# One PSUM evacuation of batch 1's convolution moved from VectorE to ScalarE

## The chip, the cores and the metric

The kernel runs on one core of a Trainium2 chip. The metric is the device time of one execution in microseconds. The engines are named as in the profile: PE is TensorE, the matrix engine (PEld its weight loads), DVE is VectorE, ACT is ScalarE, POOL is GpSimd, and SP is the engine that issues most DMAs.

## The reference

The input x is 8 batches of 4224 rows and 192 columns. First a lightweight causal convolution runs along the rows, with 7 taps and one softmax-normalised filter for each of 8 heads (24 columns each). Then a low-rank mixer works on the result:

```python
# attention part: w is softmax of weight over its 7 taps
out = np.einsum('hk,bskhg->bshg', w, x_unf)
# mixer part
xt = x.transpose(0, 2, 1)
h = xt @ U @ V
u = x + h.transpose(0, 2, 1)
ch = np.maximum(u @ w_ch1, 0.0) @ w_ch2
return (u + ch).astype(np.float32)
```

U is 4224x32, V is 32x4224, w_ch1 is 192x768 and w_ch2 is 768x192.

## The kernel before

The rows are cut into tiles of 128: 33 per batch, 264 in all, and 33 groups of 8 tiles. Work on a group has these steps, each with its line:

- The convolution makes y (tile y_sb). It multiplies banded matrices with pieces of x on TensorE and evacuates the PSUM banks to SBUF as bf16. Batches 0 and 1 use `conv` (matmuls L365); from batch 2 on `conv32` is used (matmuls L335). Both evacuate through the helper `evac`, whose ScalarE branch is L252 (an activation with Copy) and whose VectorE branch is L254 (a tensor copy). A string such as "AD" says which engine takes which half: "A" is ScalarE, "D" is VectorE.
- `tt_mm` (L398) contracts y of a whole batch with U; `tt_split` (L412, L413), `tt_sum` (L424) and `tt_done` (L418) bring the result to SBUF.
- `h_group` and `h_tiles` multiply it with V (L453) and VectorE adds y, which makes u (tile u_sb, L475). `transp` (L494) transposes u with a DMA into uT.
- `w1` multiplies uT with the first weight (L550) and evacuates with a ReLU into rl_sb, on ScalarE (L564) or VectorE (L566).
- `w2` multiplies rl_sb with the second weight (L579); VectorE adds u (L588) and SP writes the result out (L596).

All matmul outputs take one of 8 PSUM banks from a single pool (`bank()`), in turn. A bank is used again 8 allocations later, when its evacuation is over.

The order of the work is written out by hand. The list `SLOTS` (L615) gives, for each slot, groups for `w1`, groups for `w2`, and jobs to be placed between the calls of `w2`. No planner or scheduler moves anything. The third slot is `([2], [1], {0: ["d1", "h1"], 1: ["t1"], ...})`: after `w1` of group 2, and ahead of the first `w2` call of group 1, the job "d1" runs the whole convolution of batch 1, and then "h1" runs `h_group(1)`. After that first `w2` call comes "t1", `tt_mm` of batch 1. "s1" and "h4" follow later in the slot, and `w1` of group 3 opens the next slot.

The job "d1" (L761 to L764) loops over the 8 heads. For each head `conv` takes two banks and makes 8 matmuls; the first bank holds rows of 16 tiles (16 times 24 is 384 columns), the second those of 17 tiles (408 columns). The two banks are then evacuated, the first by ScalarE, the second by VectorE. After the last head the transpose of group 3, `transp(3)`, is issued, held back until the last matmul of the convolution.

Of the kernel before, what the change touches and what calls it, by code (L numbers as in the profile page):

```python
# [14 lines left out]
def kernel(  # L15
# [40 lines left out]
    def bank():  # L56
        return psp.tile([P, 512], F32, name="ps", tag="ps")
# [192 lines left out]
    def evac(eng, out, in_):  # L250
        if eng == "A":
            nc.scalar.activation(out=out, in_=in_, func=ACT.Copy)  # L252
        else:
            nc.vector.tensor_copy(out=out, in_=in_)  # L254
# [27 lines left out]
    def x_shift(b):  # L282


        xbt[b] = xbs.tile([P, NB1, D], BF16, name="xb_sb")

        def same(s0, s1, *rest):
            def step():
                nc.gpsimd.tensor_copy(out=xbt[b][:, s0:s1, :], in_=xt[b][:, s0 + 1 : s1 + 1, :])  # L289
                for t0, t1 in rest:  # L290
                    nc.gpsimd.tensor_copy(
                        out=xbt[b][HB : HB + QB, t0:t1, :],
                        in_=xt[b][HB : HB + QB, t0 + 1 : t1 + 1, :],
                    )

            return step

        def ahead(r, s0, s1):
            def step():
                q = slice(HB * r + QB, HB * r + HB)  # L300
                nc.gpsimd.tensor_copy(out=xbt[b][q, s0:s1, :], in_=xt[b][q, s0:s1, :])  # L301

            return step

        m = NB0 // 2
        return [
            same(0, m),
            same(m, NB0, (NB0, NB1)),
            ahead(0, 0, m),
            ahead(0, m, NB0),  # L310
            ahead(1, 0, m),
            ahead(1, m, NB1),
        ]
# [3 lines left out]
    def conv32(b, h0, nh, engs):  # L317


        if yt[b] is None:  # L320
            yt[b] = ys.tile([P, NT, D], BF16, name="y_sb")
        nk = (NB0 // 2, NB1 // 2)
        for n in range(nh):
            h = h0 + n
            hs = slice(h * GS, h * GS + GS)
            pp = [bank(), bank()]
            for cg in range(4):
                t, w, st = (
                    (xt[b], bands[h // HQ][:, h % HQ, QB : 2 * QB], 1 + cg // 2)
                    if cg % 2  # L330
                    else (xbt[b], band2[:, h, :], cg // 2)
                )
                for r in range(2):
                    hr = slice(HB * r, HB * r + HB)
                    nc.tensor.matmul(  # L335
                        out=pp[r][QB * cg : QB * cg + QB, 0 : nk[r] * GS],
                        lhsT=w[hr],
                        rhs=t[hr, st : st + 2 * nk[r] - 1 : 2, hs],
                        start=True,
                        stop=True,  # L340
                        tile_position=(HB * r, QB * cg),
                    )
            for part in range(2):
                j0 = NB0 // 2 * part
                evac(
                    engs[(2 * n + part) % len(engs)],
                    yt[b][:, j0 : j0 + nk[part], hs],
                    pp[part][:, 0 : nk[part] * GS].rearrange("p (k a) -> p k a", a=GS),
                )

    def conv(b, h0, nh, rs, engs, k0=0, k1=NT, pp=None):

        if yt[b] is None:
            yt[b] = ys.tile([P, NT, D], BF16, name="y_sb")
        nk = {r: min(k1, (NB0, NB1)[r] // 2) - k0 for r in rs}
        if pp is None:
            pp = {r: bank() for r in rs}
        w = nh * GS
        for hh in range(nh):
            h = h0 + hh  # L360
            for halo in range(2):
                for r in rs:
                    for c in range(2):
                        st = 1 - halo + c + 2 * k0
                        last = nc.tensor.matmul(  # L365
                            out=pp[r][HB * c : HB * c + HB, 0 : nk[r] * w].rearrange(
                                "p (k a) -> p k a", a=w
                            )[:, :, hh * GS : hh * GS + GS],
                            lhsT=bands[h // HQ][
                                HB * r : HB * r + HB, h % HQ, HB * halo : HB * halo + HB  # L370
                            ],
                            rhs=xt[b][
                                HB * r : HB * r + HB,
                                st : st + 2 * nk[r] - 1 : 2,
                                h * GS : h * GS + GS,
                            ],
                            start=(halo == 0),
                            stop=(halo == 1),
                            tile_position=(HB * r, HB * c),
                        )  # L380
        for n, r in enumerate(rs):
            j0 = NB0 // 2 * r + k0
            evac(
                engs[n % len(engs)],
                yt[b][:, j0 : j0 + nk[r], h0 * GS : h0 * GS + w],
                pp[r][:, 0 : nk[r] * w].rearrange("p (k a) -> p k a", a=w),
            )
        return last
# [3 lines left out]
    def tt_mm(b, js, p=None):  # L392

        if p is None:
            p = bank()
        for n, j in enumerate(js):
            c = n % 4
            nc.tensor.matmul(  # L398
                out=p[32 * c : 32 * c + 32, 0:D],
                lhsT=U_sb[:, j // 4, j % 4, :],  # L400
                rhs=yt[b][:, j, :],
                start=(n < 4),
                stop=(n + 4 >= len(js)),
                tile_position=(0, 32 * c),
            )
        return p

    def tt_split(b, p):

        hi = sml.tile([P, D], BF16, name="tt_hi")  # L410
        lo = sml.tile([P, D], BF16, name="tt_lo")
        nc.scalar.activation(out=hi[:], in_=p[:, 0:D], func=ACT.Copy)  # L412
        nc.vector.tensor_tensor(out=lo[:], in0=p[:, 0:D], in1=hi[:], op=ALU.subtract)  # L413
        ttb[b] += [hi, lo]
# [6 lines left out]
    def tt_sum(b):  # L421
        p = bank()
        for n, part in enumerate(ttb[b]):
            nc.tensor.matmul(  # L424
                out=p[:, 0:D],
                lhsT=R4[:],
                rhs=part[:],
                start=(n == 0),
                stop=(n + 1 == len(ttb[b])),
            )  # L430
        tt_done(b, p)
# [52 lines left out]
    def h_group(g):  # L484
        t0, t1 = g * GT, g * GT + GT
        while t0 < t1:
            b = t0 // NT
            te = min(t1, (b + 1) * NT)
            h_tiles(b, t0 - b * NT, te - b * NT)
            t0 = te  # L490

    def transp(g):
        uTt[g] = uts.tile([P, 4, 3, P], BF16, name="uT")
        return nc.sync.dma_start_transpose(  # L494
            out=uTt[g][:].rearrange("p i c t -> p (i c) t"),
            in_=ut[g][:].rearrange("p i c f k -> p (i c f k)"),
        )
# [100 lines left out]
    def held(ins, after):  # L598
        tc.add_manual_dep(
            ins.ins,  # L600
            after.ins.name,
            mybir.DependencyInfo(mybir.DependencyClass.Sync, mybir.DependencyReason.DATA),
            reason="transfer held back",
        )

    def x_load(b, q, after):
        if q == 0:
            x_tile(b)
            x_zero(b, nc.gpsimd)
        held(x_part(b, *XP[q]), after)  # L610
# [145 lines left out]
    def do(what):  # L756
        if what[0] == "c":
            b, h0, n, engs = what[1:].split(":")
            conv32(int(b), int(h0), int(n), engs)
            return  # L760
        if what[0] == "d":  # L761
            for h in range(H):
                last = conv(int(what[1:]), h, 1, [0, 1], "AD")
            held(transp(3), last)  # L764
            return
        if what[0] == "l":
            b, q = (int(v) for v in what[1:].split(":"))
            x_load(b, q, done_w2[-1])
            return
        if what[0] == "x":  # L770
            b, n = (int(v) for v in what[1:].split(":"))
            steps.extend(x_shift(b))
            for _ in range(n):
                steps.pop(0)()
            return
        n = int(what[1:])
        if what[0] == "h":
            h_group(n)
            if n > 1 and n != 3:
                transp(n)  # L780
        elif what[0] == "t":
            tt_split(n, tt_mm(n, range(NT)))
        else:
            tt_sum(n)
# [55 lines left out]
```

## Time and profile before

| what | value |
|---|---|
| median of 8 runs | 326.55 us (326.29 to 326.89) |
| the profiled execution | 326.5 us |
| its span, first to last instruction | 324.7 us |
| granted TensorE clock, mean | 0.997 |
| instructions | 9590 |
| conv evacuations of batch 1 on ACT (L252, 128x384) | 8, from 38.28 us, 3.19 us together |
| conv evacuations of batch 1 on DVE (L254, 128x408) | 8, from 38.43 us, 4.00 us together |

Times inside the trace count from the first instruction. The profiled execution's own time is 1.8 us longer than its span, for what lies around the span. A line of the timeline has the start in us, the length in us, the engine, the line of the kernel, the operation, what is written and read, the shape and the count; in square brackets stands how long the engine was idle before it and what released it. A line of the groups ends with busy us, mean ns of one, and idle us before them. A line of the waits has who waited for whom, the total in us, how often, and the longest. The chain that ended last is followed back from the last instruction, at each step to what released it.

### The profile page before, as it was taken

The numbers are of one execution on the slowest core, as the hardware profiler recorded it, in microseconds if no ns is written. First come the engines' busy times: TensorE is split into PE (matmuls) and PEld (weight loads), VectorE is DVE, ScalarE is ACT, GpSimd is POOL, SyncE is SP. The second block draws the span as 40 slices with busy tenths as digits, with TensorE's granted clock in tenths as the row PEclk, the third lists the DMA queues.
The fourth block names the chain that finished last, engine by engine and source line by source line (L and its number), as shares of the span: only waits on it lengthen the run. The fifth ranks groups of instructions, "written<-read, shape, count | busy, mean of one in ns | idle before, by whom it ended". The sixth has DMA issues, their size and how long they took to land.

```text
span 324.7 us, 9590 instructions
## 1 busy us (share of the span) xinstructions
PE 318.1 (98%) x3998; PEld 223.9 (69%) x3998; DVE 269.5 (83%) x552; ACT 170.1 (52%) x343; POOL 143.6 (44%) x112
## 2 busy tenths in 40 slices
PE   8999999999999999999999999999999999999994
PEld 3757576478678647866864784597796497497494
DVE  7769999987977986998798699879888888896853
ACT  1766724860874396098249609825804903903900
POOL 8684179729937794685779496000000000000000
PEclk9999999999999999999999999999999999999998
DMA  9999993999996899699889966149077089048044
GB/s 106 192 191 183 210 199 106 197 196 246 219 150 182 222 177 169 165 145 202 189 219 158 216 173 168 51 120 249 26 199 240 3 164 275 2 121 269 2 142 151
DMA packets 122908, 53.52 MB, mean 165 GB/s; under 512 B 87761, under 2 KB 122833, under 8 KB 122865
## 3 DMA queue, kind: packets, MB, share of 16 engines
q1 hardware_dynamic: 84528, 38.08, 47.1%
q0 software_dynamic: 38192, 14.73, 39.8%
q8 instruction: 31, 0.51, 0.7%
q14 instruction: 13, 0.10, 0.1%
q10 hardware_dynamic: 144, 0.10, 0.1%
HBM read 29.49 MB, written 25.95 MB: 171 GB/s over the span
## 4 chain that ended last, share of the span: by engine, by line
PE 94%; DVE 3%; ACT 1%; issue 0%
PE ps L579 42%; PE ps L550 39%; PE ps L335 3%; PE ps L453 3%; PE ps L155 2%; PE ps L398 2%; DVE rl_sb L566 1%; PE ps L365 1%; ACT rl_sb L564 1%; DVE y_sb L254 1%; DVE u_sb L475 1%; PE ps L505 1%; PE ps L520 0%; DVE band L254 0%; PE ps L678 0%; PE ps L424 0%
## 5 line engine op out<-in xcount | busy, mean ns | idle before, releaser
L564 ACT ACTIVATE rl_sb<-ps 128x512 bf16<-128x512 f32 x233 | 124.3, 604 | 108.0 <-PE ps L550 96.0
L579 PE MATMUL ps<-W_sb,rl_sb 128*128 128x192 bf16 x1584 | 141.9, 246 | 0.1
L579 PEld LDWEIGHTS <-rl_sb 128*128 128x128 bf16 x1584 | 128.0, 98 | 13.5 <-issue 13.0
L550 PE MATMUL ps<-uT,W_sb 64*128 64x512 bf16 x1188 | 131.7, 376 | 0.0
L566 DVE TENSOR_SCALAR rl_sb<-ps 128x512 bf16<-128x512 f32 x163 | 105.3, 687 | 15.7 <-PE ps L550 15.4
L550 PEld LDWEIGHTS <-W_sb 64*128 64x128 bf16 x1188 | 66.8, 94 | 60.6 <-issue 4.0
L588 DVE TENSOR_TENSOR out_sb<-ps,u_sb 128x384 f32<-128x384 f32 (+1 forms) x133 | 70.3, 549 | 25.8 <-PE ps L579 25.4
L301 POOL COPY xb_sb<-x_sb 32x3072 bf16<-32x3072 bf16 (+1 forms) x24 | 67.5, 2824 | 0.7
L475 DVE TENSOR_TENSOR u_sb<-y_sb,ps 128x192 bf16<-128x192 bf16 (+1 forms) x168 | 66.2, 460 | 0.0
L289 POOL COPY xb_sb<-x_sb 128x3072 bf16<-128x3072 bf16 x12 | 32.7, 2742 | 36.0 <-PE ps L335 21.5
L252 ACT ACTIVATE y_sb<-ps 128x408 bf16<-128x408 f32 (+4 forms) x89 | 37.8, 513 | 10.4 <-PE ps L335 7.8
L79 POOL DMA_DIRECT2D x_sb<-in_x_dram x32 | 27.0, 847 | 16.2 <-PE ps L550 9.4
L254 DVE CAST y_sb<-ps 128x408 bf16<-128x408 f32 (+4 forms) x37 | 19.7, 577 | 0.8 <-PE ps L365 0.7
L453 PE MATMUL ps<-tt_sb,V_sb 32*128 32x192 bf16 x264 | 12.4, 246 | 0.2 <-DVE y_sb L254 0.2
L335 PE MATMUL ps<-xb_sb,band 64*32 64x384 bf16 x192 | 12.1, 332 | 0.0
L335 PE MATMUL ps<-x_sb,band 64*32 64x384 bf16 x192 | 12.1, 333 | 0.0
L453 PEld LDWEIGHTS <-V_sb 32*128 32x128 bf16 x264 | 4.7, 92 | 7.5 <-issue 7.5
L155 PE MATMUL ps<-zz 128*128 128x512 f32 x12 | 7.5, 778 | 1.5 <-DVE zz L145 1.5
L412 ACT ACTIVATE tt_hi<-ps 128x192 bf16<-128x192 f32 x8 | 2.6, 330 | 11.2 <-PE ps L398 11.1
L365 PE MATMUL ps<-x_sb,band 64*64 64x240 bf16 (+3 forms) x192 | 8.0, 275 | 0.4 <-DVE band L254 0.4
L365 PEld LDWEIGHTS <-band 64*64 64x64 bf16 x192 | 6.0, 106 | 2.2 <-issue 1.2
L335 PEld LDWEIGHTS <-band 64*32 64x32 bf16 x384 | 4.5, 89 | 4.1 <-issue 3.0
(65 smaller groups left out, 72.9 us busy)
## 6 DMA issues: line engine op xcount, KB each, us to landing
out_dram<-out_sb SPq DMA_DIRECT2D x131, 192.0 KB, 3.0
x_sb<-in_x_dram POOLq DMA_DIRECT2D x14, 384.0 KB, 7.6
x_sb<-in_x_dram POOLq DMA_DIRECT2D x7, 432.0 KB, 8.2
x_sb<-in_x_dram POOLq DMA_DIRECT2D x7, 408.0 KB, 8.9
x_sb<-in_x_dram POOLq DMA_DIRECT2D x1, 504.0 KB, 7.5
uT<-u_sb SPq DMA_TRANSPOSE x31, 3.8
x_sb<-in_x_dram POOLq DMA_DIRECT2D x1, 480.0 KB, 5.6
W_sb<-in_moe_w_ch_dram POOLq DMA_DIRECT2D x2, 192.0 KB, 7.6
```

The lines of the kernel that those rows point to most:

```text
L79: return nc.gpsimd.dma_start(out=xt[b][HB * r : HB * r + HB, s0:s1, :], in_=x[b, blk * HB : (blk + s1 - s0) * HB, :].rearrange("(j p) d -> ...
L252: nc.scalar.activation(out=out, in_=in_, func=ACT.Copy)
L289: nc.gpsimd.tensor_copy(out=xbt[b][:, s0:s1, :], in_=xt[b][:, s0 + 1 : s1 + 1, :])
L301: nc.gpsimd.tensor_copy(out=xbt[b][q, s0:s1, :], in_=xt[b][q, s0:s1, :])
L335: nc.tensor.matmul(out=pp[r][QB * cg : QB * cg + QB, 0 : nk[r] * GS], lhsT=w[hr], rhs=t[hr, st : st + 2 * nk[r] - 1 : 2, hs], start=True, ...
L453: nc.tensor.matmul(out=banks[pr][:, a * D : (a + 1) * D], lhsT=V_sb[32 * q : 32 * q + 32, (j // 8) * 2 + j % 2, :], rhs=ttb[b][32 * q : 32 ...
L475: nc.vector.tensor_tensor(out=u_group(g)[:, i : i + n, :, hf, :], in0=yt[b][:, run[0] : run[0] + n, :].rearrange("p n (c k) -> p n c k", c=3),
L550: last = nc.tensor.matmul(out=pps[m][hf][:], lhsT=W1_sb[HB * hf : HB * hf + HB, c, m * P : (m + 1) * P], rhs=uTt[g][HB * hf : HB * hf + HB ...
L564: nc.scalar.activation(out=rl[:, m, hf, :], in_=pp[hf][:], func=ACT.Relu)
L566: nc.vector.tensor_scalar_max(out=rl[:, m, hf, :], in0=pp[hf][:], scalar1=0.0)
L579: last = nc.tensor.matmul(out=cps[:, a * D : (a + 1) * D], lhsT=rlt[g][:, m, hf, (i + a) * P : (i + a + 1) * P], rhs=W2_sb[:, m, :], start ...
L588: nc.vector.tensor_tensor(out=o[:, 0:n, :].rearrange("p n (c k) -> p n c k", c=3), in0=cps[:, 0 : n * D].rearrange("p (n c k) -> p n c k", ...
```

## The change

The call of `conv` inside the job "d1" gets another string for head 2 alone. For that head both halves are evacuated by ScalarE, so that ScalarE takes nine of the sixteen evacuations of batch 1 and VectorE seven.

```diff
         if what[0] == "d":
             for h in range(H):
-                last = conv(int(what[1:]), h, 1, [0, 1], "AD")
+                last = conv(int(what[1:]), h, 1, [0, 1], "AA" if h == 2 else "AD")
             held(transp(3), last)
             return
```

The matmuls, the banks, the order of the heads and the transpose are as they were.

## The prediction

> **What bounds the kernel now.** I read the busy shares first, then the chain that ended last, then TensorE's waits, then the timeline around the convolution of batch 1.
>
> The page, busy shares and the chain:
> ```profile
> PE 318.1 (98%) x3998; PEld 223.9 (69%) x3998; DVE 269.5 (83%) x552; ACT 170.1 (52%) x343; POOL 143.6 (44%) x112
> ...
> PE 94%; DVE 3%; ACT 1%; issue 0%
> ```
> TensorE holds the end. Relief of VectorE counts only where TensorE waits for VectorE. TensorE's own waits are few:
> ```profile
> PE ps L155 <- DVE zz L145: 1.5, 1, 1.5
> PE ps L365 <- DVE band L254: 0.4, 1, 0.4
> PE ps L453 <- DVE y_sb L254: 0.2, 1, 0.2
> ```
> The columns are total us, times, longest. The third is the only one that the conv of batch 1 causes. The chain of waits from 36 to 48 us (start, length, what) shows where it sits:
> ```profile
> 36.53 1.99 DVE rl_sb L566 x3
> 38.51 2.95 DVE y_sb L254 x6
> 41.46 0.04 issue
> 41.50 0.32 PE ps L453 x5
> 41.82 1.10 PE ps L579 x12
> 42.92 0.85 PE ps L398 x33
> ```
> Here VectorE's evacuations release the chain, and then TensorE takes it back and keeps it. The timeline of that stretch gives both engines:
> ```profile
> 37.69 3.37 PE L365 MATMUL ps<-x_sb,band 64*64 64x384 bf16 x64
> 38.28 3.19 ACT L252 ACTIVATE y_sb<-ps 128x384 bf16<-128x384 f32 x8
> 38.43 4.00 DVE L254 CAST y_sb<-ps 128x408 bf16<-128x408 f32 x8
> ...
> 41.09 1.52 SPq L494 DMA_TRANSPOSE uT<-u_sb  x1
> 41.50 0.32 PE L453 MATMUL ps<-tt_sb,V_sb 32*128 32x192 bf16 x5 [0.23 <-DVE y_sb L254]
> ```
> ScalarE ends its eight at 41.47, VectorE at 42.43. There are eight PSUM banks and two to a head, so heads 4 to 7 reuse the banks of heads 0 to 3; h_group(1) (L453) takes the four banks of heads 4 and 5, and the next w2 call (L579) the first bank of head 6. L453 stood 0.23 us until VectorE had emptied head 5's second bank.
>
> **The change, part by part.** Nothing is added or removed in count: one 128x408 evacuation, head 2's second half, goes from VectorE's queue to ScalarE's.
>
> VectorE: its eight follow each other every 0.489 us (first start 38.43, last end 42.43, one 0.571 long: (4.00 - 0.571)/7 = 0.49). From head 3 on each comes 0.49 us earlier, if its matmuls are done, which they are: head 5's begin by 39.55, and VectorE reaches head 5 only at 40.39 even then.
>
> ScalarE: single rows give the price.
> ```profile
> 40.50 0.58 ACT L252 ACTIVATE y_sb<-ps 128x384 bf16<-128x384 f32 x1
> 67.84 0.51 ACT L252 ACTIVATE y_sb<-ps 128x408 bf16<-128x408 f32 x1
> 68.23 0.52 ACT L252 ACTIVATE y_sb<-ps 128x408 bf16<-128x408 f32 x1
> ```
> ScalarE's first conv evacuation ends at 38.78, the seventh (head 6) at 40.50 + 0.58 = 41.08: one every 0.383 us. Two neighbouring 128x408 end at 68.35 and 68.75, 0.40 apart. The added one therefore delays each later evacuation on ScalarE by 0.40 us. Bounds: 0.39 (their starts, 67.84 to 68.23) to 0.58 (the longest single ScalarE evacuation of this stretch, if nothing overlapped). I take 0.40, since the neighbouring pair is the same instruction in the same kind of backlog.
>
> New times by bank, with 0.055 us from an evacuation's end to the matmul (VectorE's 41.45 to 41.50):
> - head 6, second bank: freed by ScalarE at 39.55 + 0.40 = 39.95, where VectorE freed it at 39.98. No change worth counting.
> - head 7, first bank: head 3 on ScalarE, 39.93 + 0.40 = 40.34, so its matmuls begin at 40.39; today head 7 is held to 40.53 by its second bank. Gain there 0.14.
> - L453, first: head 4 on ScalarE, 40.32 + 0.40 = 40.72; third: head 5 on ScalarE, 40.70 + 0.40 = 41.10, so 41.16. The fourth, head 5 on VectorE, is free at 41.45 - 0.49 = 40.96. The stall that ended at 41.50 now ends at 41.16.
> - L579: 0.25 us after that by its distance today (41.50 to 41.76), thus 41.41, but its bank is head 6's on ScalarE, 41.08 + 0.40 = 41.49, plus 0.055: 41.54. Today 41.76. **Gain 0.22 us.** So VectorE's wait is replaced by a shorter one for ScalarE, and less than half of VectorE's 0.49 us arrives.
>
> What is late next: L398 of batch 1 reads all sixteen pieces. ScalarE's last one would end at 41.47 + 0.40 = 41.87, VectorE's at 41.94, and TensorE comes there at 42.85 - 0.22 = 42.63. Covered by 0.7 us. Behind the added instruction on ScalarE stand only its own conv pieces and then tt_hi, before which it idles 2.3 us today (waiting for L398), so 0.40 is hidden there. Behind it on VectorE the u_sb and out_sb work starts 0.49 us earlier, but from 45.9 VectorE waits for L579 again (0.41 us), so only TensorE's lead is passed on. The transpose that is held on the last conv matmul issues some 0.14 us earlier; nothing else moves on SP, and on POOL nothing.
>
> Downstream TensorE's rows have no wait on a DMA at all, so the lead should survive to the end. The profiled execution took 326.5 us (span 324.7, 1.8 around it): 324.7 - 0.22 + 1.8 = 326.28. The median of the runs is 326.55, 0.05 above the profiled one; I keep the profiled base and write **326.3**.
>
> [...] The rows show 0.51 us for one alone, but 0.40 between ends, since neighbours overlap.
>
> **Rivals.** A fifth of a percent, 0.65 us, is about what a measurement of this kernel can tell from no change; around 326.5 that is 325.85 to 327.15.
>
> *Absorbed, 326.5.* If a later wait runs by its own clock, the lead ends there. For it: POOL's batch-2 copies (L289) wait 8.4 us for their x load. Against: they end with the last L301 at 59.7, and the conv that reads them begins at 66.9. Also here is a ScalarE price at its upper bound, 0.58: gain 0.04.
>
> *VectorE's whole half microsecond arrives, 326.0.* VectorE is 2.00 of 2.00 us busy in each stretch from 38 to 44 us. If its backlog, not the named bank, sets TensorE's pace up to 45 us, 0.49 is gained. Against: the next L453 and L579 banks are ScalarE's, and TensorE is unbroken from 41.76.
>
> *Slower: the transpose, up to 328.7.* uT of group 3 is issued at 41.09 and lands 5.4 us later, 46.5; L550 of that group starts at 47.29, so 47.07 with the lead. Issued at 40.95, it holds L550 up if it lands more than 6.1 us later, and the kernel is slower from 6.3. Between 28 and 70 us the slowest took 8.5: 49.45, a stall of 2.4, net 2.2 us slower. For it: DMA is 9 in every slice, and x loads take 86% of the engines' time from 36 to 42 us. Against: an earlier issue into the same queue seldom lands later.
>
> That the change doesn't do what it says has little room: the order on each engine is written by hand and the source has nine to seven.
>
> **How the numbers follow.** Forecast (0.1 to 0.4 us gained) 0.62; absorbed 0.17; VectorE's whole relief 0.12; transpose late 0.09. Executions of one kernel spread 326.29 to 326.89, so 0.2 us of scatter stands on every case. The range leaves out the transpose's far end and the edge of the third: 325.95 to 326.75. Faster by over 0.2% takes half of the third case, 0.06; slower by over 0.2% most of the last, 0.07; the rest, 0.87, is within 0.2%.
>
> **What would show it.** Right: in the conv stretch ScalarE shows nine L252 and VectorE seven L254, ending within 0.1 us of each other near 41.9; L453's 0.23 us wait on VectorE is gone, in its place a wait on ScalarE's y_sb, of about 0.1 us; L579 first starts near 41.54 and L550 of group 3 near 47.07. Wrong: L579 not before 41.7 (ScalarE's price above 0.55); L550 of group 3 waiting on a DMA; or the lead present at 47 and missing at 81.3, where today a 108-matmul L550 run starts.

## The result and the profile after

The changed kernel takes 325.54 us (median of 20 runs, 324.92 to 326.32) beside 326.77 us for the kernel before (median of 58 runs). The ratio is 0.9955, with a 95% interval of 0.9945 to 0.9965. So by the ratio it is faster by 0.45%, some 1.5 us (the two medians differ by 1.23 us), where 0.22 us had been forecast and 325.95 was the lower end of the range.

The profiled execution took 325.59 us, with a span of 323.8 us. The page of the changed kernel, busy shares and the chain:
```profile
PE 318.4 (98%) x3998; PEld 224.0 (69%) x3998; DVE 269.1 (83%) x551; ACT 170.5 (53%) x344; POOL 143.5 (44%) x112
...
PE 94%; ACT 3%; DVE 2%; issue 0%
```
One instruction has gone from DVE (552 before) to ACT (343 before), and the chain now passes through ACT where it passed through DVE. TensorE's waits in the changed kernel:
```profile
PE ps L155 <- DVE zz L145: 1.5, 1, 1.5
PE ps L365 <- DVE band L254: 0.4, 1, 0.4
```
The wait of L453 on VectorE is gone. The timeline of the conv of batch 1 after the change:
```profile
38.19 3.24 PE L365 MATMUL ps<-x_sb,band 64*64 64x384 bf16 x64
38.78 3.59 ACT L252 ACTIVATE y_sb<-ps 128x384 bf16<-128x384 f32 x9
38.93 3.51 DVE L254 CAST y_sb<-ps 128x408 bf16<-128x408 f32 x7
...
41.36 0.63 PE L453 MATMUL ps<-tt_sb,V_sb 32*128 32x192 bf16 x8
```
The two engines now end together, at 42.37 and 42.44. This execution is 0.50 us later than the one of before when the stretch starts (38.19 against 37.69), so only distances can be compared. The first L579 behind the conv, in the timeline of the kernel before:
```profile
41.76 1.16 PE L579 MATMUL ps<-W_sb,rl_sb 128*128 128x192 bf16 x12
```
The chain of waits from 36 to 48 us of the changed kernel gives the same point there:
```profile
38.90 3.10 ACT y_sb L252 x8
42.00 0.04 issue
42.04 1.15 PE ps L579 x12
```
From the first conv matmul to the first L579 it is 42.04 - 38.19 = 3.85 us, and it was 41.76 - 37.69 = 4.07. That is 0.22 us less, as forecast. The lead stays: from that L579 to the end of the last matmul it is 278.59 us in the trace of before and 278.58 in that of after.

The rest came **behind TensorE's last matmul**, where I had not looked. That matmul ends at 320.35 before and at 320.62 after. So the tail (span less that end) is 4.36 us before and 3.19 us after: 1.17 us less. With the 0.22 this makes 1.39 us of the 1.5. (The two profiled spans differ by 0.9 us only, because the execution of after reached the conv 0.50 us later.)

Stretches of the tail, kernel before. Behind the colon the row has the length of the stretch, then busy us of PE, PEld, DVE, ACT and POOL, the granted clock, the DMA share and GB/s:
```profile
321.00:322.00 1.00, 0.00 (x0) 0.00 (x0) 0.00 (x0) 0.00 (x0) 0.00 (x0) 1.00 1.06 345
322.00:323.00 1.00, 0.00 (x0) 0.00 (x0) 0.00 (x0) 0.00 (x0) 0.00 (x0) 0.91 0.08 21
323.00:324.00 1.00, 0.00 (x0) 0.00 (x0) 0.00 (x0) 0.00 (x0) 0.00 (x0) 0.50 0.01 4
```
All engines are done by 321, the DMA engines nearly so by 322, and then 0.08 of sixteen engines, about one engine, works on until 323.2. The same stretches after the change:
```profile
321.00:322.00 1.00, 0.00 (x0) 0.00 (x0) 0.01 (x1) 0.00 (x0) 0.00 (x0) 1.00 0.90 302
322.00:323.00 1.00, 0.00 (x0) 0.00 (x0) 0.00 (x0) 0.00 (x0) 0.00 (x0) 1.00 0.32 100
```
Here the output packets all end by 322.36 (by the packet records); only the packet described below runs on, to 322.98. The DMA issues of the last microseconds, before (KB each, us to landing):
```profile
out_dram<-out_sb SPq DMA_DIRECT2D x1, 96.0 KB, 2.9
out_dram<-out_sb ACTq DMA_DIRECT2D x1, 96.0 KB, 2.8
```
and after:
```profile
out_dram<-out_sb SPq DMA_DIRECT2D x1, 96.0 KB, 1.7
out_dram<-out_sb ACTq DMA_DIRECT2D x1, 96.0 KB, 1.7
```
The two last output transfers land 1.1 to 1.2 us sooner. What stood beside them is an instruction transfer. DMA queues from 321.0 to 321.5 us of the kernel before (packets, MB, share of 16 engines):
```profile
q1 hardware_dynamic: 237, 0.17, 102.6%
q14 instruction: 1, 0.01, 9.1%
```
One packet of 8 KB of instructions took 0.73 us of a DMA engine's time (0.091 x 16 x 0.5 us). By its record it starts at 321.12, that is 0.77 us after the last matmul, while the outputs are under way, and ends at 321.84. From 321.94 on four output packets take 0.10 to 0.12 us each in place of 0.036, and behind them a single file of packets of 0.036 us ends at 323.18. The records don't name the DMA engine of a packet; that these stood behind the instruction packet on one engine is my inference from the single file. The packet's own 0.73 us and the four slow packets (some 0.3 us more than usual) come near the 1.17 us of the tail; the rest isn't traced. In the changed kernel the packet comes at 322.30, 1.68 us after the last matmul, when the outputs are all but written, less than 0.1 us before the end of the last one.

### The profile page after: what moved, and what is told of

It is laid out like the page before. It is cut to its first block, busy times and chain, and to the rows that moved or that the text cites. A ratio compares the mean times of both kernels' runs of the same rounds, so it can differ in the third digit from the quotient of the medians.

```text
span 323.8 us, 9590 instructions
## 1 busy us (share of the span) xinstructions
PE 318.4 (98%) x3998; PEld 224.0 (69%) x3998; DVE 269.1 (83%) x551; ACT 170.5 (53%) x344; POOL 143.5 (44%) x112
## 4 chain that ended last, share of the span: by engine, by line
PE 94%; ACT 3%; DVE 2%; issue 0%
PE ps L579 42%; PE ps L550 39%; PE ps L335 3%; PE ps L453 3%; PE ps L155 2%; PE ps L398 2%; ACT rl_sb L564 2%; PE ps L365 1%; ACT y_sb L252 1%; DVE u_sb L475 1%; DVE rl_sb L566 1%; PE ps L520 0%; PE ps L505 0%; DVE band L254 0%; PE ps L678 0%; PE ps L424 0%
## 5 line engine op out<-in xcount | busy, mean ns | idle before, releaser
L579 PE MATMUL ps<-W_sb,rl_sb 128*128 128x192 bf16 x1584 | 141.9, 246 | 0.2
L579 PEld LDWEIGHTS <-rl_sb 128*128 128x128 bf16 x1584 | 128.1, 98 | 13.5 <-issue 13.1
L550 PE MATMUL ps<-uT,W_sb 64*128 64x512 bf16 x1188 | 131.7, 376 | 0.0
L550 PEld LDWEIGHTS <-W_sb 64*128 64x128 bf16 x1188 | 66.8, 94 | 60.5 <-issue 3.7
L252 ACT ACTIVATE y_sb<-ps 128x384 bf16<-128x384 f32 (+4 forms) x90 | 38.2, 515 | 10.4 <-PE ps L335 7.8
L453 PE MATMUL ps<-tt_sb,V_sb 32*128 32x192 bf16 x264 | 12.4, 246 | 0.1
L453 PEld LDWEIGHTS <-V_sb 32*128 32x128 bf16 x264 | 4.7, 92 | 7.3 <-issue 7.3
```

What stands on the lines that cost most here:

```text
L453: nc.tensor.matmul(out=banks[pr][:, a * D : (a + 1) * D], lhsT=V_sb[32 * q : 32 * q + 32, (j // 8) * 2 + j % 2, :], rhs=ttb[b][32 * q : 32 ...
L550: last = nc.tensor.matmul(out=pps[m][hf][:], lhsT=W1_sb[HB * hf : HB * hf + HB, c, m * P : (m + 1) * P], rhs=uTt[g][HB * hf : HB * hf + HB ...
L579: last = nc.tensor.matmul(out=cps[:, a * D : (a + 1) * D], lhsT=rlt[g][:, m, hf, (i + a) * P : (i + a + 1) * P], rhs=W2_sb[:, m, :], start ...
```

## The experiments

Two theories. **Fetch**: 0.22 us from the banks of the conv, and 1.2 us because VectorE, with one instruction fewer by the end, draws its last 8 KB of instructions at another moment and no longer beside the last outputs. **Conv**: all of the gain comes from the better balance in batch 1 and spreads from there.

The numbers of all kernels first, by VectorE's instructions relative to before. "conv" is the distance from the first matmul of batch 1 to the first L579 behind it, "fetch" the start of the 8 KB packet after the end of the last matmul, "tail" the span less that end, all in us from one profiled execution each; the ratio is to the kernel before, with its interval.

| kernel | DVE count | ACT count | conv | fetch | tail | ratio |
|---|---|---|---|---|---|---|
| before | 0 | 0 | 4.07 | 0.77 | 4.36 | 1 |
| before_again | 0 | 0 | 4.07 | 0.72 | 4.19 | one execution, 327.11 us |
| place_alone | 0 | 0 | 3.86 | 0.71 | 4.24 | 0.9998 (0.9979 to 1.0017) |
| act_plus_one | 0 | +1 | 4.07 | 0.76 | 4.21 | 1.0042 (1.0019 to 1.0064) |
| act_plus_clean | 0 | +1 | 4.07 | 0.75 | 4.08 | 1.0001 (0.9987 to 1.0015) |
| dve_restored | 0 | +1 | 3.85 | 0.71 | 4.29 | 0.9992 (0.9976 to 1.0007) |
| after | -1 | +1 | 3.85 | 1.68 | 3.19 | 0.9955 (0.9945 to 0.9965) |
| after_again | -1 | +1 | 3.86 | 1.66 | 3.20 | 0.9957 (0.9940 to 0.9975) |
| count_elsewhere | -1 | +1 | 4.07 | 1.66 | 3.20 | 0.9969 (0.9950 to 0.9989) |
| dve_minus_one | -1 | 0 | 4.07 | 1.65 | 3.21 | 0.9952 (0.9936 to 0.9969) |
| head7_on_act | -1 | +1 | 4.07 | 1.78 | 3.20 | 0.9966 (0.9952 to 0.9981) |
| head2_and_6 | -1 | +1 | 3.79 | 1.67 | 4.23 | 0.9967 (0.9949 to 0.9984) |
| dve_plus_two | +2 | 0 | 4.07 | 0.63 | 4.02 | 0.9984 (0.9972 to 0.9995) |
| dve_plus_eight | +8 | 0 | 4.07 | -2.74 | 3.19 | 0.9953 (0.9938 to 0.9968) |

The executions of every kernel scatter by about 1 us. Part of it shows: the first conv matmul of batch 0 starts anywhere from 9.3 to 10.8 us in these profiles. Another part lies between 80 and 90 us. From the first L579 to the end of the last matmul nine profiles have 278.58 to 278.60 us, but before_again, act_plus_one, act_plus_clean and dve_restored have 278.83 to 279.18 and head2_and_6 has 280.06. In these five the transpose that is issued at 67.4 to 68.5 us took 9.8 to 11.0 us to land, in the other nine 7.7 to 9.4. Four of the five have VectorE's count of before; whether the count has a part in this was not tried, and a part of the ratios may come from here. So the tail and the conv distance are read from the traces, and the ratios only bear them out.

**before_again**: the kernel before, with no edit.

> The kernel before, unchanged, profiled once more. Fetch theory (an 8 KB instruction transfer, issued at 321.1 us as the last outputs are written, holds up one DMA engine): the same fetch falls again within 1 us after TensorE's last matmul, and the span ends 4.2 to 4.5 us after that matmul. Chance theory (the late landing of one execution): the tail may be short, 3.1 to 3.4 us, in this execution.

The fetch came 0.72 us after the last matmul, the tail was 4.19 us, at the edge of what was expected. The long tail is no chance of one execution.

**after_again**: the changed kernel, with no edit.

> The changed kernel, unchanged, beside the kernel before on one chip. Fetch theory: 1.2 to 1.5 us faster again, the tail after the last matmul 3.1 to 3.3 us, and the 8 KB fetch after the last output has landed. Chance theory: about 0.2 us faster, which is what the stretch of the convolution shows, with a tail that varies from one execution to the next.

Ratio 0.9957, tail 3.20, fetch at 1.66. This repeats the result and the tail, but the packet did not wait for the last output: that landed 2.09 us after the last matmul, and its last packets were being written as the instruction packet started.

**count_elsewhere**: the counts of the changed kernel, with the conv of batch 1 left alone.
```diff
-                2: [f"c{b}:3:3:AAD"],
+                2: [f"c{b}:3:3:" + ("AADAAA" if b == 7 else "AAD")],
```

> The convolution of batch 1 as before (eight and eight); one evacuation of the convolution of batch 7 (head 5, second half) goes from VectorE to ScalarE, where TensorE waits for neither, so each engine has as many instructions by the end as in the changed kernel. Fetch theory: 0.9 to 1.3 us faster than before, nearly the whole of the result, with the conv of batch 1 as slow as before and a tail of 3.1 to 3.4 us. Conv theory (all of the gain comes from the balance in batch 1 and spreads from there): within 0.2 us of before.

Faster by 0.31% (0.9969), some 1.0 us, with the conv at 4.07 as before. The last output transfers of this kernel:
```profile
out_dram<-out_sb SPq DMA_DIRECT2D x1, 96.0 KB, 1.7
out_dram<-out_sb ACTq DMA_DIRECT2D x1, 96.0 KB, 1.7
```
They land in 1.7 us as in the changed kernel, though batch 1 is untouched. The conv theory falls: most of the gain is to be had without its cause.

**place_alone**: the changed kernel's batch 1, with the counts of before.
```diff
-                last = conv(int(what[1:]), h, 1, [0, 1], "AD")
+                last = conv(int(what[1:]), h, 1, [0, 1], "AA" if h == 2 else "AD")
...
-                2: [f"c{b}:3:3:AAD"],
+                2: [f"c{b}:3:3:" + ("AADADD" if b == 7 else "AAD")],
```

> Batch 1 as in the changed kernel (nine and seven), and one evacuation of batch 7 (head 5, first half) goes from ScalarE to VectorE, so each engine has as many instructions by the end as before the change. Fetch theory: 0.15 to 0.3 us faster than before, tail 4.2 to 4.5 us after the last matmul. Conv theory: 1.2 to 1.5 us faster, as the changed kernel.

The conv distance is 3.86, so the 0.22 us are there, and the tail is 4.24. The ratio, 0.9998 with 0.0019 to each side, can't tell 0.2 us from nothing, but it excludes the 1.2 to 1.5 us of the conv theory.

**act_plus_one**: one more instruction on ScalarE, none less on VectorE.
```diff
-    nc.vector.memzero(zz[:])
+    nc.vector.memzero(zz[:]); dmy = cst.tile([P, 1], F32, name="dmy")
...
-            held(transp(3), last)
+            held(transp(3), last); nc.scalar.activation(out=dmy[:], in_=zz[:, 0:1], func=ACT.Copy)
```

> The kernel before, with one added instruction on ScalarE (a copy of one column that nothing reads, behind the conv of batch 1, where ScalarE idles 2.3 us); VectorE has as many instructions as before. If the position of VectorE's last 8 KB fetch sets the tail: as before, within 0.2 us, tail 4.2 to 4.5 us after the last matmul. If ScalarE's position sets it: 0.9 to 1.3 us faster, tail 3.1 to 3.4 us.

The tail stayed at 4.21 and the fetch at 0.76, so one more instruction on ScalarE did not move the fetch (0.77 before). But the kernel was slower by 0.42%, which neither side expected.

**act_plus_clean**: the same without the new tile.
```diff
-            held(transp(3), last)
+            held(transp(3), last); nc.scalar.activation(out=zz[:, 0:1], in_=zz[:, 1:2], func=ACT.Copy)
```

> As act_plus_one, but the added copy on ScalarE writes a column of a tile that is there already, so no tile is added and no address moves. VectorE-fetch theory: within 0.25 us of before, tail 4.2 to 4.5 us. If act_plus_one was slow because of an added ScalarE instruction by itself: again about 1 us slower than before.

Ratio 1.0001, tail 4.08 (a little under the range): an added ScalarE instruction costs nothing that can be measured here. So act_plus_one's 0.42% isn't the price of the instruction by itself. The added tile, which may have moved the tiles behind it, is the difference in the kernels; the two were also measured on different chips, each beside the kernel before. How the tile would cost time was not tried, and the cause of the 0.42% stays open.

**dve_minus_one**: VectorE's count alone.
```diff
-    rq = cst.tile([P, 2], F32, name="rq")
-    for r in range(4):
+    rq = cst.tile([P, 2], F32, name="rq"); nc.vector.memset(rq[0:QB, :], 0.0)
+    for r in range(1, 4):
```

> The kernel before, with one instruction fewer on VectorE (two small memsets of zeros at the start are made as one); ScalarE as before. If the position of VectorE's last fetch sets the tail: 0.9 to 1.3 us faster, tail 3.1 to 3.4 us, with the conv of batch 1 as slow as before (4.07 us from its first matmul to the first L579). If ScalarE's position sets it: as before, within 0.2 us.

Ratio 0.9952, tail 3.21, conv 4.07 as before. Two memsets made into one in the first microseconds shorten the tail by 1.15 us, nearly all of the change's gain. DMA queues from 322.0 to 322.5 us of this kernel show where the packet has gone (it starts at 322.27):
```profile
q14 instruction: 1, 0.01, 7.6%
```

**dve_restored**: the changed kernel, with VectorE's count brought back.
```diff
-        t = g * GT + t0
+        t = g * GT + t0; t0 == 0 and g == 24 and nc.vector.tensor_copy(out=zz[:, g : g + 1], in_=zz[:, 500:501])
```

> The changed kernel with one added instruction on VectorE (a copy of one column that nothing reads, in group 24, where VectorE waits for L579), so VectorE's count is again that of before while the conv of batch 1 keeps nine and seven. VectorE-fetch theory: 0.9 to 1.3 us slower than the changed kernel, 0.1 to 0.3 us faster than before, tail 4.2 to 4.5 us, 3.85 us from the first conv matmul to the first L579. If the fetch were not the cause: as the changed kernel, 1.2 us faster than before.

The tail is back at 4.29 and the fetch at 0.71, with the conv at 3.85. The ratio is 0.9992 (0.9976 to 1.0007): one small copy, made where VectorE waits anyway (25.4 us for L579 in all, by the page of before), took the gain of the tail away. The conv's 0.22 us shows in the trace; the ratio can't tell it from nothing.

**dve_plus_two** and **dve_plus_eight**: the copy of dve_restored in the kernel before, in groups 24 and 25 (`24 <= g < 26`), and in groups 24 to 31 (`24 <= g < 32`).

> The kernel before with two such copies on VectorE (groups 24 and 25). VectorE-fetch theory: the fetch comes one out_sb step earlier, 0.3 to 0.9 us, and beside earlier output transfers: tail 3.3 to 4.2 us, time between before and the changed kernel. If the fetch were not the cause: as before.

> The kernel before with eight such copies on VectorE (groups 24 to 31). VectorE-fetch theory: the fetch comes some four out_sb steps, 3 to 4.5 us, earlier, well ahead of the last outputs: tail 3.1 to 3.4 us, 0.8 to 1.2 us faster than before in spite of eight more instructions. If fewer instructions are faster by themselves: as before or slower.

With two, the fetch came only 0.14 us earlier than in the trace of before, less than expected, and the tail was 4.02: the time lies between, 0.9984. Its packet took 0.31 us by its record, and the tail was still 0.8 us longer than the short ones, so the packet's own length doesn't set the loss. With eight, the packet is found from 318.0 to 318.5 us, ahead of the last outputs:
```profile
q14 instruction: 1, 0.01, 6.2%
```
and the last outputs land in 1.7 us, tail 3.19, ratio 0.9953. Eight more instructions make the kernel as fast as one fewer (0.9953 and 0.9952). So here it is the moment of the fetch that counts, and not how much VectorE has to do.

**head7_on_act**: the changed kernel with `h == 7` in place of `h == 2`.

> As the changed kernel, but head 7 gives its second half to ScalarE in place of head 2, so the counts are those of the changed kernel, and the moved evacuation comes too late to free the banks that L453 and L579 wait for. Bank theory of the 0.22 us: 4.07 us from the first conv matmul to the first L579, as before. If a lighter VectorE were enough: 3.85 us. Fetch theory: short tail, 3.1 to 3.4 us, so 0.9 to 1.3 us faster than before in either case.

The conv distance is 4.07, and TensorE's waits hold the old row again:
```profile
PE ps L453 <- DVE y_sb L254: 0.2, 1, 0.2
```
The relief of VectorE after the banks of heads 4 to 6 are claimed is worth nothing to TensorE, as the bank theory has it. The tail is short (3.20) since the counts are those of the changed kernel.

**head2_and_6**: the changed kernel with head 6 exchanged, in an attempt to beat both.
```diff
-                last = conv(int(what[1:]), h, 1, [0, 1], "AA" if h == 2 else "AD")
+                last = conv(int(what[1:]), h, 1, [0, 1], "AA" if h == 2 else "DA" if h == 6 else "AD")
```

> The changed kernel, and head 6 with its halves exchanged (VectorE takes the first, ScalarE the second), so that the bank that L579 waits for is freed by VectorE, which is 0.05 us ahead there. Bank theory: 3.78 to 3.83 us from the first conv matmul to the first L579, 0.03 to 0.07 less than in the changed kernel. Fetch theory: tail 3.1 to 3.4 us, so 1.2 to 1.5 us faster than before.

The conv distance is 3.79, 0.06 us less than in the changed kernel, as expected. The time doesn't show it: 325.44 us median of 10, and a ratio of 0.9967 whose interval covers the changed kernel's 0.9955. Its profile is of the longest of its executions (327.77 us) and its tail of 4.23 us is the one exception in the table. Here the packet, though as late as in the changed kernel, started ahead of a last 4-byte packet, which its record puts 0.5 us behind the others; the remainder of that tail is not explained. So a packet at 1.67 us is no warrant of a short tail: it starts while the last packets are written. The same execution lost 1.4 us around 82 us, where a transpose of uT took 11.0 us to land (7.7 for the same one in the trace of after).

## Why the prediction was wrong

**Right, step by step.** The price of the moved evacuation on ScalarE (0.40 us; its nine took 3.59 us where the eight took 3.19), the banks that it delays, and the exchange of VectorE's wait for a shorter one on ScalarE gave a gain of 0.22 us; the trace has 0.22, and place_alone and dve_restored show it with the counts of before (3.86 and 3.85). L579 was forecast for 41.54; less the 0.50 us by which this execution runs later, it came at 41.54. L550 of group 3 was forecast for 47.07 and came at 47.06 on the same scale. head7_on_act (4.07 us) shows that the banks, and not VectorE's load, are the cause. (39.93 + 0.40 was written as 40.34, a rounding without effect.) The lead was carried to the last matmul, so neither "absorbed" nor the late transpose of group 3 happened in these two traces. That an earlier issue seldom lands later held here: the transpose of group 3 was issued at 41.48, on the scale of before 0.11 us earlier, and landed 5.2 us later (5.4 before), and in both traces SP's 164 transfers landed in the order of their issue. In one point it was off: the wait on ScalarE that was to take the place of L453's is in the chain, but not in the list of waits.

**The step that failed** is the base of the sum, "324.7 - 0.22 + 1.8". It takes the 4.36 us behind the last matmul for fixed. "Nothing else moves on SP, and on POOL nothing" looked at the instructions of the queues and left out the instructions themselves as traffic. The page of before had it in a row, "q14 instruction: 13, 0.10, 0.1%", and the two last outputs' landing of 2.8 and 2.9 us beside a median of 2.0 for the three before them was the sign that something stood in their way. The missing term is the change of the tail, 1.17 us between the two traces, and dve_minus_one (0.9952) shows it by itself. That the tail became shorter was luck: nothing in the change aimed at it, and one VectorE instruction put back (dve_restored) undoes it. None of the rivals named it. "VectorE's whole half microsecond" reached 326.0 by another mechanism, and the measured 325.54 is no support for it: the conv gave 0.22 and not 0.49 us.

TensorE's list of waits names no instruction packet in either trace, though q8 moved 31 of them (0.51 MB, 16 KB each) and q14 13 (0.10 MB, 8 KB each). At the end it is otherwise: with the one beside the last outputs the tail is 4.36 us in the trace of before, and 3.21 in dve_minus_one, where it comes 0.9 us later.

**Still open.** That the packet belongs to VectorE's stream rests on the counts: -1 delays it by about 0.9 us, +8 brings it forward by 3.5, and ScalarE's +1 leaves it (0.76 and 0.75 beside 0.77). The trace's instructions bear it out: as the packet starts, VectorE has begun 704 recorded instructions in the kernel before and also 704 in dve_plus_eight, where it is 3.5 us earlier (703 in the changed kernel, 706 in dve_plus_two). Why +2 moved it by so little was not found. What releases it in the changed kernel was not found: it starts within 0.1 us after SP's first wait for the last landings, and VectorE has no recorded instruction there. Why head2_and_6's tail was long with the packet in the same place, and how often that happens in other executions, is open too.

## What to carry to other kernels

When one instruction is moved between engines, count each engine's instructions to the end of the program and see in the trace where instruction packets fall against the last output transfers; what follows the last matmul is part of the sum, and here it was no constant (4.36 us in one trace, 3.19 in the other). A gain or loss of a microsecond that no stretch of the body accounts for should be looked for in the landing of the last transfers (here 2.8 and 2.9 us beside 1.7). To tell a true gain from such a shift, put the same count somewhere harmless, and bring the count back in the changed kernel; the traces of these two runs show it, where the times alone may be too coarse.

## What the runs showed of the hardware

One 8 KB instruction packet beside the last outputs (0.57 to 0.79 us long by its record) made the kernel's end about 1 us later, in all six profiled kernels whose VectorE count was that of before (tails of 4.08 to 4.36 us). Where it came 0.9 us later or 3.5 us earlier, six of seven tails were 3.19 to 3.21 us; head2_and_6 (4.23) is the exception. In the trace of before VectorE started a conv evacuation of batch 1 (128x408) every 0.49 us, and ScalarE ended one every 0.38 us (128x384), or 0.40 (128x408, at 68 us), although single rows read 0.57 and 0.50 to 0.58; here the sums for the backlog came out with the distances between ends.
